# A fused scan and mixture-of-adapters kernel: the order of every engine written out instead of planned, and 17 instead of 21 gate products on GpSimd

## The chip, the cores and the metric

The kernel runs on one core of one Trainium2 chip. The metric is the device time of one execution in microseconds; lower is better. Five engines work side by side from their own instruction lists: TensorE (PE: matrix products and transposes), VectorE (DVE), ScalarE (ACT), GpSimd (POOL) and SyncE (SP, which here only starts transfers). They meet only at semaphores.

## What is computed

A recurrence over each of 8 sequences of 6400 steps, 128 channels wide, and then a small mixture of experts on its result; two of eight experts are taken for each of the 51,200 rows.

```python
h = a[:, t] * h + b[:, t]; out[:, t] = h          # the scan; x = out, as (51200, 128)
logits = x @ w_gate                               # (51200, 8)
topk = np.argpartition(-logits, 2, axis=1)[:, :2]
w = softmax of the two chosen logits
delta[rows with e chosen] += w * ((x @ A[e]) @ B[e])   # A: 128x16, B: 16x128 for each e
return x + delta
```

## The kernel before

The 51,200 rows are 100 units of 512 rows. Each unit goes through the same steps, which the code names by a letter and the number of the unit; in the profile they are found by line and tile:

- **AB** (TensorE, L86, pA and pB): 8 pairs of float32 transposes bring a unit of `a` and of `b` into PSUM with the channels on the partitions. At the edges a unit has a step A of its own for `a`.
- **aev** (ScalarE, L491): pA is copied to a_st. **scan** (VectorE, L510): one hardware scan over 512 columns, from a_st and pB into the ring xT (16 units). Units in which a new sequence starts are scanned in two pieces.
- **L** (TensorE, L82, into pTL): the logits, 4 matmuls with 8 columns. **Z** (L82, pZ): x times all 8 A side by side, 4 matmuls with 128 columns.
- The gating steps, for a group of units at once (mostly 4, fewer at both ends): **lev** (ScalarE, L583) copies the logits out, **mx** (L589) or **m1** and **m2** (L618, L646) on VectorE find the two largest, **p1** to **p7** (mostly GpSimd, L599 to L674) build the mask and the difference, **sig** (ScalarE, L684) is the sigmoid that gives the weights g.
- **mul** (L729): Z times the gate, into zw. On VectorE straight from PSUM; for some units on GpSimd, which then reads a copy **zev** (ScalarE, L715) of pZ in SBUF.
- **T** (TensorE, L86, pTL): 4 transposes of zw; **tev** (ScalarE, L786) copies them out. **R** (L82, pO from xT and ident_h): x itself is brought back to rows, 4 matmuls; **D** (L82, pO from zwT): plus zw times B.
- **oev** (L821): pO is copied to outt, on ScalarE, for some of the last 10 units on VectorE. **st** (SP): a store of 512 KB for two units, 256 KB for one.
- Loads **lda**, **ldb** (SP, L311), 512 KB for two units, go through rings of 8 slots each; a load may start when the AB steps that read its slot are done.

pA has one PSUM bank, pB, pZ and pO two each, pTL one that L and T share in turns. So AB of unit w waits for aev of unit w-1 and the scan of unit w-2, T of v for tev of v-1, R of v for oev of v-2.

What sets the order: every step is added to `_Plan` with a cost and a key (its unit plus an offset `KEY` by kind, L13). `schedule` (L108) is a list scheduler: it keeps a clock for each engine and takes, within a `SLACK`, the step with the smallest key. Its result is a fixed instruction list for each engine with the waits that the data and the buffers ask for. In the middle of the kernel that list repeats one pattern on TensorE, for each unit w:

```
AB(w) T(w-12) L(w-2) D(w-14) Z(w-9) R(w-13) AB(w+1) ...
```

`HOLD = 22` with `FREE = 100` ties the store of units u, u+1 to the scan of unit u+22, for u+22 below FREE (L847 to L851). `POOL_MULS = (2, 10, 4, 2)` puts mul of units 6, 10, 14 to 86 on GpSimd, 21 of them. TensorE's program is cut into parts of 243 instructions, with a branch in between (`_Parts`).

Of the kernel before, what the change touches and what calls it, by code (L numbers as in the profile page):

```python
# [12 lines left out]
KEY = {  # L13
    "AB": -228.9, "aev": 79.1, "scan": 140.1, "L": -12.2, "lev": -63.6, "gate": 83.5, "sig": 69.7, "Z": 27.8,
    "mul": -75.3, "zev": 6.2, "T": -117.7, "tev": 38.1, "R": 189.8, "D": 29.2, "oev": 168.4,
}
SLACK = {"pe": 20.0, "dve": 20.0, "act": 0.0, "pool": 60.0, "sp": 120.0}
# [3 lines left out]
POOL_MULS = (2, 10, 4, 2)  # L21
HOLD = 22
FREE = 100
HEATS = 7
WIDE = 100
SOLO = (2, 4)
FUSE = (100, 100)
WIDE8 = 460.0
# [4 lines left out]
FILLS = 0  # L33


class _Op:


    def __init__(self, name, engs, kind, unit, cost, emit, deps, dma, bank, mode):
        self.name = name  # L40
        self.engs = engs
        self.eng = engs[0]
        self.kind = kind
        self.unit = unit
        self.cost = cost
        self.emit = emit
        self.deps = deps
        self.dma = dma
        self.bank = bank
        self.mode = mode  # L50
        self.signal = False
        self.done = None
# [7 lines left out]


# [30 lines left out]
class _Plan:  # L92


    def __init__(self, sems, offset, slack):
        self.sems = sems
        self.offset = offset
        self.slack = slack
        self.ops = {}
        self.order = {e: [] for e in sems}  # L100

    def add(self, name, eng, kind, unit, cost, emit, deps=(), dma=None, bank=None, mode=None):

        engs = (eng,) if isinstance(eng, str) else eng
        cost = cost if isinstance(cost, dict) else {e: cost for e in engs}
        self.ops[name] = _Op(name, engs, kind, unit, cost, emit, list(deps), dma, bank, mode)

    def schedule(self, first, link, landing, switch):  # L108
        ops = self.ops
        users = {n: [] for n in ops}  # L110
        left = {}
        for op in ops.values():
            op.deps = [ops[d] for d in dict.fromkeys(op.deps) if d in ops]
            left[op.name] = len(op.deps)
            op.key = op.unit + self.offset.get(op.kind, 0.0)
            op.quick = min(c[0] for c in op.cost.values())
        for op in ops.values():
            for d in op.deps:
                users[d.name].append(op)
        begin, end = {}, {}  # L120
        cand = {e: [] for e in self.sems}
        free = {e: first for e in self.sems}
        bank = {}
        mode = None
        for op in ops.values():
            if not left[op.name]:
                for e in op.engs:
                    cand[e].append((0.0, op))
        todo = len(ops)
        while todo:  # L130
            found, soonest = [], {}
            for e, c in cand.items():
                for x in c:
                    op = x[1]
                    t = max(free[e], x[0])
                    if op.bank:
                        for o in bank.get(op.bank, {}).values():
                            if o.eng != e:
                                t = max(t, end[o.name])
                    if op.mode and mode and op.mode != mode:  # L140
                        t = max(t, free[e] + switch)
                    t += op.cost[e][0] - op.quick
                    found.append((t, op, e, x))
                    if t < soonest.get(e, 1e18):
                        soonest[e] = t
            e0 = min(soonest, key=soonest.get)
            limit = soonest[e0] + self.slack.get(e0, 0.0)
            t, op, e, pick = min((f for f in found if f[2] == e0 and f[0] <= limit), key=lambda f: (f[1].key, f[0]))
            t -= op.cost[e][0] - op.quick
            for x in op.engs:  # L150
                cand[x].remove(pick)
            op.eng = e
            mode = op.mode or mode
            if op.bank:
                held = bank.setdefault(op.bank, {})
                op.deps += [o for o in held.values() if o.eng != e]
                held[e] = op
            self.order[e].append(op)
            begin[op.name] = t
            free[e] = t + op.cost[e][0]  # L160
            if op.dma:
                ready = free[e] + 1000.0
                wait = max(0.0, link - ready)
                link = max(link, ready) + op.dma[2]
                end[op.name] = link + 300.0 + min(wait, landing(link))
            else:
                end[op.name] = t + op.cost[e][1]
            todo -= 1
            for u in users[op.name]:
                left[u.name] -= 1  # L170
                if not left[u.name]:
                    for x in u.engs:
                        cand[x].append((max(end[d.name] for d in u.deps), u))
        self.begin, self.end = begin, end
        self.span = max(end.values())
        for op in ops.values():
            for d in op.deps:
                d.signal = True
        for e, seq in self.order.items():
            n = 0  # L180
            for op in seq:
                if op.dma:
                    op.done = op.dma[:2]
                else:
                    n += op.signal
                    op.done = (self.sems[e], n)
# [18 lines left out]
def bass_associative_scan_2x2__then__mixture_of_adapters_kernel(  # L205
# [20 lines left out]
    lo, hi, every, at = POOL_MULS  # L226
    ON_POOL = lambda v: lo < v < NU - hi and v % every == at
# [22 lines left out]
    with ExitStack() as stack:  # L250
# [45 lines left out]
        s_cst = sb(nc.semaphore("s_cst"))  # L296
        dma_sem = {}

        plan = _Plan(sems, KEY, SLACK)
        add = plan.add  # L300

        def add_dma(name, eng, unit, starts, slot, time, deps=()):
# [11 lines left out]
            add(name, eng, "dma", unit, (450.0 * len(starts), 0.0), emit, deps, (sem, value, time))  # L314


        add("id0", "pool", "fix", -109, (200.0, 450.0), lambda h: h.memset(ident_f[:, :], 0.0))
# [3 lines left out]
            "fix",  # L321
            -109,
            (300.0, 400.0),
# [9 lines left out]
            ["id0"],  # L333
        )

        def cst_load(name, dst, src, after):

            sem = sb(nc.semaphore(f"s_{name}"))
            add(
                name,  # L340
                "act",
                "fix",
                -109,
                (450.0, 0.0),
                lambda h: h.dma_start(dst, src).then_inc(sem, 16),
                after,
                (sem, 16, 100.0),
            )
# [9 lines left out]
        add("w0", "dve", "fix", -109, (60.0, 200.0), lambda h: h.memset(warm[:, :], 0.0))  # L358
        add("table", "act", "fix", -108, (1500.0, 1600.0), lambda h: h.activation(warm[:, :], warm[:, :], ACTF.Sigmoid), ["w0"])
        add("wt", "dve", "fix", -109, (270.0, 400.0), lambda h: h.memset(warm_t[:, :], 0.0))  # L360
# [6 lines left out]
        add("heat", "pe", "fix", -109, (372.0 * HEATS, 372.0 * HEATS), heat, ["wt"], mode="half")  # L367

        def fill(w):


            def emit(h):
                for _ in range(2):
                    last = h.matmul(pO[1][:, :], warm_t[:, 0:128], warm_t[:, :])
                return last

            add(f"fill{w}", "pe", "fix", 1000.0, (440.0, 640.0), emit, [f"AB{w}"], mode="full")

        for w in range(FILLS):
            fill(w)  # L380
        add("idh", "dve", "fix", -108, (150.0, 330.0), lambda h: h.tensor_copy(ident_h[:, :], ident_f[:, :]), ["id"])
        add("cstg", "pool", "fix", -108, (190.0, 290.0), lambda h: h.tensor_copy(wg_h, cst_f[:, 0:E]), ["ld_g"])
        add(
            "cstA",
            "pool",
            "fix",
            -107,
            (290.0, 390.0),
            lambda h: h.tensor_copy(Acat_h, cst_f[:, E : E + 128]),
            ["ld_A"],  # L390
        )
        add(
            "cstB",
            "pool",
            "fix",
            -106,
            (290.0, 390.0),
            lambda h: h.tensor_copy(Bcat_h, cst_f[:, E + 128 : E + 256]),
            ["ld_B"],
        )  # L400
# [26 lines left out]
        def load(t, w):  # L427
# [3 lines left out]
            if many == 2 and n >= WIDE and n % 2 == 0 and w + 4 <= NU:  # L431
                many = 4
# [358 lines left out]
        def delta(v):  # L791
# [17 lines left out]
            if v == 1:  # L809
                deps += [f"fill{w}" for w in range(5)]  # L810
# [116 lines left out]
```

## Time and profile before

| | |
|---|---|
| median of 3 runs | 204.37 us (204.28 to 204.4) |
| the profiled execution, its own time | 204.88 us |
| its span, first to last instruction | 203.1 us |
| granted TensorE clock, mean | 0.989 |
| PE busy | 191.2 us, 3591 matmuls |
| DVE busy | 184.8 us, 268 instructions |
| ACT busy | 173.7 us |
| POOL busy | 115.7 us |
| moved by DMA | 79.35 MB, mean 391 GB/s |
| chain that ended last | PE 81%, DVE 6%, ACT 6%, DMA 2% |

"Span" leaves out 1.78 us of the execution that lie around the instructions. Matmuls overlap in the pipeline, so PE can be shown busy at every moment and still differ in how many it finishes; the count in a window, or the distance from start to start, tells more than its busy share. VectorE's and ScalarE's instructions overlap a little too (the next one starts while the last one ends), so what one costs in a full row is the distance from its start to the next start.

### The profile page before, as it was taken

To read this page: it belongs to the slowest core of one execution; us is meant where nothing else is said; L and a number is where in the kernel's file an instruction comes from. 1 tells how busy PE (TensorE), PEld (TensorE's weight loads), DVE (VectorE), ACT (ScalarE), POOL (GpSimd) and SP (SyncE) were. 2 spreads that over 40 slices of the span, in tenths; PEclk is the share of its full clock that TensorE was granted. 3 is DMA by queue.
4 is the path that set the end of the run, shared out by engine and by line. 5 is a ranking of instruction groups with operands and counts; after the bars stand their busy time and mean duration, and the time that the engine had idled before them with its cause. 6 is when DMAs were issued, how large, how long until landed. Compare 5 with 4: busy or idle time off the path is not lost.

```text
span 203.1 us, 8757 instructions
## 1 busy us (share of the span) xinstructions
PE 191.2 (94%) x3591; PEld 172.3 (85%) x3591; DVE 184.8 (91%) x268; ACT 173.7 (86%) x383; POOL 115.7 (57%) x244
## 2 busy tenths in 40 slices
PE   7788888999999999999999999999999999999992
PEld 3666777879899999999999999999999999999981
DVE  1579989999999999999999999999999999989970
ACT  3157686869899999989999999999999999999883
POOL 1324427568567466565656746656565687875520
PEclk9799999999999999999999999999999999999999
DMA  7999999999999999999999999999999999988867
GB/s 182 402 410 408 403 409 405 404 412 404 404 414 412 416 412 410 413 408 416 414 408 416 410 412 416 410 414 414 409 411 414 414 416 409 372 330 345 324 250 279
DMA packets 23688, 79.35 MB, mean 391 GB/s; under 512 B 3681, under 2 KB 3809, under 8 KB 23649
## 3 DMA queue, kind: packets, MB, share of 16 engines
q1 hardware_dynamic: 22320, 78.65, 97.0%
q8 instruction: 29, 0.48, 0.9%
q10 hardware_dynamic: 1328, 0.14, 0.5%
q14 instruction: 11, 0.08, 0.1%
HBM read 52.56 MB, written 26.21 MB: 388 GB/s over the span
## 4 chain that ended last, share of the span: by engine, by line
PE 81%; DVE 6%; ACT 6%; DMA 2%; issue 2%; POOL 1%; SPq 0%; DVEq 0%
PE pA L86 26%; PE pO L82 23%; PE pTL L86 14%; PE pZ L82 10%; PE pTL L82 5%; DVE xT L510 4%; PE pB L86 4%; DMA a_in<-in_a_dram 2%; ACT a_st L491 2%; ACT outt L821 2%; ACT zwT L786 1%; DVE mx L589 0%; SPq L311 0%; DVE zw L729 0%; ACT z_sb L715 0%
## 5 line engine op out<-in xcount | busy, mean ns | idle before, releaser
L510 DVE TENSOR_TENSOR_SCAN xT<-a_st,xT,pB 128x512 f16<-128x512 f32 x96 | 120.2, 1252 | 4.4 <-PE pZ L82 1.1
L491 ACT COPY a_st<-pA 128x512 f32<-128x512 f32 x100 | 60.6, 606 | 20.4 <-PE pB L86 15.7
L86 PE MATMUL pA<-ident_f,a_in 64*128 64x64 f32 (+1 forms) x792 | 71.8, 230 | 3.3 <-DMA a_in<-in_a_dram 1.1
L86 PE MATMUL pB<-ident_f,b_in 64*128 64x64 f32 (+1 forms) x792 | 72.5, 232 | 0.2
L86 PEld LDWEIGHTS pA<-ident_f,a_in 64*128 64x128 f32 (+1 forms) x792 | 58.0, 139 | 11.6 <-issue 2.4
L821 ACT COPY outt<-pO 128x512 f32<-128x512 f32 x96 | 59.5, 626 | 1.9 <-PE pO L82 1.7
L786 ACT COPY zwT<-pTL 128x512 f16<-128x512 f16 x95 | 58.4, 615 | 1.0 <-PE pTL L86 1.0
L86 PEld LDWEIGHTS pB<-ident_f,b_in 64*128 64x128 f32 (+1 forms) x792 | 58.0, 140 | 0.7 <-DMA b_in<-in_b_dram 0.4
L729 DVE TENSOR_TENSOR zw<-pZ,g 128x512 f16<-128x512 f32 x79 | 53.2, 679 | 2.1 <-PE pTL L86 1.2
L82 PE MATMUL pO<-ident_h,xT 128*128 128x128 f16 x400 | 41.2, 229 | 0.9 <-ACT outt L821 0.9
L82 PE MATMUL pZ<-cst_h,xT 128*128 128x128 f16 x400 | 38.6, 221 | 0.0
L86 PE MATMUL pTL<-ident_h,zw 128*128 128x128 f16 x380 | 37.7, 222 | 0.4 <-ACT zwT L786 0.4
L82 PE MATMUL pO<-cst_h,zwT 128*128 128x128 f16 x400 | 36.9, 218 | 0.6 <-ACT zwT L786 0.4
L82 PEld LDWEIGHTS pO<-ident_h,xT 128*128 128x128 f16 x400 | 32.8, 148 | 1.6 <-ACT outt L821 1.2
L729 POOL TENSOR_TENSOR zw<-z_sb,g 128x512 f16<-128x512 f32 x21 | 22.3, 1060 | 17.6 <-PE pTL L82 17.2
L82 PE MATMUL pTL<-cst_h,xT 128*128 128x8 f16 x400 | 27.9, 175 | 1.6 <-DVE xT L510 1.3
L82 PEld LDWEIGHTS pZ<-cst_h,xT 128*128 128x128 f16 x400 | 28.1, 115 | 0.2
L86 PEld LDWEIGHTS pTL<-ident_h,zw 128*128 128x128 f16 x380 | 21.8, 98 | 6.4 <-ACT zwT L786 0.5
L82 PEld LDWEIGHTS pTL<-cst_h,xT 128*128 128x128 f16 x400 | 23.6, 117 | 2.9 <-DVE xT L510 1.8
L625 POOL TENSOR_TENSOR d<-Lg,m 128x128 f32<-128x128 f32 (+3 forms) x29 | 10.7, 368 | 26.6 <-DVE m L618 26.5
L82 PEld LDWEIGHTS pO<-cst_h,zwT 128*128 128x128 f16 x400 | 23.9, 98 | 1.0 <-PE pO L82 0.9
L660 POOL TENSOR_SCALAR pn<-d 128x128 f32<-128x128 f32 (+3 forms) x31 | 17.3, 557 | 2.7
(36 smaller groups left out, 137.2 us busy)
## 6 DMA issues: line engine op xcount, KB each, us to landing
a_in<-in_a_dram SPq DMA_DIRECT2D x49, 512.0 KB, 13.7
b_in<-in_b_dram SPq DMA_DIRECT2D x49, 512.0 KB, 13.5
out_dram<-outt SPq DMA_DIRECT2D x47, 512.0 KB, 13.1
out_dram<-outt SPq DMA_DIRECT2D x6, 256.0 KB, 2.7
a_in<-in_a_dram SPq DMA_DIRECT2D x2, 256.0 KB, 9.2
b_in<-in_b_dram SPq DMA_DIRECT2D x2, 256.0 KB, 4.3
cst_f<-in_moe_A_dram ACTq DMA_DIRECT2D x1, 64.0 KB, 4.0
cst_f<-in_moe_B_dram ACTq DMA_DIRECT2D x1, 64.0 KB, 5.0
```

What stands on the lines that cost most here:

```text
L82: return self.h.matmul(*args, **kw)
L86: return self.h.transpose(*args)
L491: lambda h: h.copy(a_st[w % 2][:, :], pA[0][:, :]),
L510: last = h.tensor_tensor_scan(out=x_at(lo, hi), data0=a_st[w % 2][:, lo:hi], data1=pB[w % 2][:, lo:hi], initial=init, op0=ALU.mult, op1=AL ...
L625: lambda h: h.tensor_tensor(out=v(d1[s]), in0=v(Lg[s]), in1=bc(m1[s]), op=ALU.subtract),
L660: lambda h: h.tensor_scalar(v(pn[s]), v(d2[s]), 0.0, -1.0e30, ALU.is_lt, ALU.mult),
L729: lambda h: h.tensor_tensor(out=oview, in0=zview, in1=gview, op=ALU.mult),
L786: lambda h: h.copy(*evacuated(v)),
L821: return copy(outt[:, v % NOUT, :], pO[v % NO][:, :])
```

## The change

The planner goes. Each engine's order is written out as a string, one letter for a step (`CODES`); steps of one kind are taken by rising unit. The order in which T/tev and L/lev share the bank pTL is written as well (`BANKS`), and so is which steps go to VectorE where there is a choice (`ELSE`). What is computed, the tiles and their sizes stay. Cut to its core:

```diff
-KEY = {"AB": -228.9, "aev": 79.1, "scan": 140.1, ...}
-SLACK = {"pe": 20.0, "dve": 20.0, "act": 0.0, "pool": 60.0, "sp": 120.0}
-POOL_MULS = (2, 10, 4, 2)
-FREE = 100
-SOLO = (2, 4)
+CODES = dict(zip("bdfkpqrvhyBCEijAacsLZuTtRDozlx41567gm23nwe",
+    "idz id ld_g ld_A ld_B w table wt heat idh cstg cstA cstB lda ldb A AB aev scan L Z mul T tev R D oev zev lev mx p4 p1 p5 p6 p7 sig m1 p2 p3 m2 st end".split()))
+ORDERS = {
+    "pe": """
+        hAaAaLaLRaZaLLTaZZLaLRaDTaZaLLDTLaZTZaRRDaTDRaLLLRLaZTZaDDLaRTZaLRLTLaZZDDTLaZRTaZDLTRaLDZTRaLTZRaTL
...
+    "dve": """
+        qvyssxsx157susxsmususmnsusnmsusnsusmsusnsusmusunsussumususnsusmsusnsusumsusnsusumsususnsusmususnussm
...
+    "act": """
+        fpkccrlclcgcglcltcglctcocltcgotcoctgoclcgtzcooctcltgcotcotcztocotgcltctooctocztlcogoctctoctocltgoczt
...
+    "sp": """
+        ijijjijijiiijjjjjiiiiijjjiijiiijjjjiijwijjiwijwijwjwjwwjjjiiiiwjiijwiiwiwwwwwjjjjwjiwwjiwiijijwwwiij
+        ijijijjjjjiiwwjwiwjwiiwwijjiwwwijiwwwwwwwwwwwwwwwwwwwe
...
+ELSE = "oev90 oev93 oev95 oev97 oev98 p5_0 p7_0 p1_1".split()
+POOL_MULS = (7, 12, 17, 22, 27, 32, 37, 42, 47, 52, 57, 62, 67, 72, 77, 82, 87)
+FREE = 90
+PAIRS = (2, 98)
+SINGLE = 2
...
-    def schedule(self, first, link, landing, switch):
...
+    def arrange(self):
+        ops = list(self.ops.values())
+        for op in ops:
+            op.deps = [self.ops[d] for d in dict.fromkeys(op.deps) if d in self.ops]
+        self.order = {e: self.pick(ORDERS[e], [op for op in ops if op.eng == e]) for e in self.sems}
+        for name, codes in BANKS.items():
+            held = {}
+            for op in self.pick(codes, [op for op in ops if op.bank == name]):
+                op.deps += [o for e, o in held.items() if e != op.eng]
+                held[op.eng] = op
...
-    ON_POOL = lambda v: lo < v < NU - hi and v % every == at
+    ON_POOL = lambda v: v in POOL_MULS
...
-            deps = [f"aev{w - 1}", f"scan{w - 2}", "id"]
+            deps = [f"aev{w - 1}", f"scan{w - 2}", "id", "heat"]
...
-            stores.append((u, len(mates(u))))
-            u += stores[-1][1]
+            n = 2 if u < NU - SINGLE else 1
+            stores.append((u, n))
+            u += n
```

In the built programs both have 3591 matmuls. VectorE gets four products more (83 instead of 79) and five of the last output copies instead of four; ScalarE loses four copies of pZ and one output copy. ScalarE's list has one table load more: before, the load for the sigmoid and a one-column sigmoid stand ahead of all copies; after, a table load stands ahead of aev0 and the one for the sigmoid, with that one-column sigmoid, stands between aev1 and lev0. Units 96 and 97 become a pair, and stores 0 to 50 replace 0 to 52.

In the middle of the kernel TensorE's list no longer repeats one pattern: between two AB steps there are three to seven others, in changing order (`AB34 Z25 R21 T23 D20 AB35 D21 Z26 T24 R22 AB36 D22 Z27 L33 T25 L34 R23 AB37`).

More of the change, by code (lines that the diff above doesn't have):

```diff
@@ L108, in schedule @@
-    def schedule(self, first, link, landing, switch):
[L109 to L176, printed above, removed]
```

282 lines of the change are left out of this document (100 added, 182 removed).

## The prediction

> **What bounds the kernel now.** I read the table of stretches first, then the order of starts on TensorE and VectorE in the middle, then both ends. The stretches are from and to, length, then PE, PEld, DVE, ACT, POOL busy us with counts, granted clock, DMA share, GB/s:
>
> ```profile
> 0.00:20.00 20.00, 15.78 (x201) 11.81 (x203) 12.40 (x35) 9.13 (x22) 5.33 (x24) 0.91 0.95 349
> 20.00:40.00 20.00, 17.48 (x338) 15.03 (x335) 19.06 (x26) 14.62 (x33) 10.34 (x26) 1.00 1.02 405
> 40.00:60.00 20.00, 19.42 (x377) 17.46 (x378) 19.60 (x27) 17.21 (x39) 13.45 (x24) 1.00 1.03 408
> 60.00:160.00 100.00, 99.96 (x1989) 92.35 (x1986) 97.90 (x128) 95.64 (x209) 62.24 (x111) 1.00 1.03 412
> 160.00:180.00 20.00, 20.00 (x398) 18.50 (x398) 19.57 (x31) 19.33 (x48) 15.37 (x39) 1.00 0.99 396
> 180.00:204.00 24.00, 18.56 (x304) 17.15 (x304) 16.27 (x26) 17.79 (x39) 8.94 (x23) 0.96 0.74 289
> ```
>
> From 60 to 180 TensorE is never idle and finishes 2387 matmuls in 120 us, 19.9 per us; a unit has 36, so a unit takes 1.81 us. In the first 60 us it finishes 916, which at that rate are 46 us of work: 14 us are missing, the start before the first data among them. From 180 on, 304 matmuls are 15.3 us of work. So TensorE sets the pace of the middle, and what an order can win lies in the first 60 us and in the last 20. VectorE is busy 95 to 98% from 20 us on, so in the first part it is VectorE that TensorE waits for.
>
> Start by start, one unit on TensorE (AB, T, L, D, Z, R, next AB):
>
> ```profile
> 80.16 0.27 PE L86 MATMUL pA<-ident_f,a_in 64*128 64x64 f32 x1
> ...
> 80.81 0.40 PE L86 MATMUL pTL<-ident_h,zw 128*128 128x128 f16 x4
> 81.04 0.28 PE L82 MATMUL pTL<-cst_h,xT 128*128 128x8 f16 x4
> 81.17 0.38 PE L82 MATMUL pO<-cst_h,zwT 128*128 128x128 f16 x4
> 81.39 0.39 PE L82 MATMUL pZ<-cst_h,xT 128*128 128x128 f16 x4
> 81.62 0.41 PE L82 MATMUL pO<-ident_h,xT 128*128 128x128 f16 x4
> 81.96 0.27 PE L86 MATMUL pA<-ident_f,a_in 64*128 64x64 f32 x1
> ```
>
> AB 0.65, T 0.23, L 0.13, D 0.22, Z 0.23, R 0.34: 1.80 us, with no idle time in a row. Another order of the same steps has the same sum: one AB per unit means one change from float32 to float16 and one back.
>
> VectorE in the middle:
>
> ```profile
> 87.53 1.27 DVE L510 TENSOR_TENSOR_SCAN xT<-a_st,xT,pB 128x512 f16<-128x512 f32 x1
> 88.73 0.69 DVE L729 TENSOR_TENSOR zw<-pZ,g 128x512 f16<-128x512 f32 x1
> 89.34 0.28 DVE L618 TENSOR_REDUCE m<-Lg 128x16 f32<-128x128 f32 x1
> 89.54 1.27 DVE L510 TENSOR_TENSOR_SCAN xT<-a_st,xT,pB 128x512 f16<-128x512 f32 x1
> ```
>
> In a full row a scan takes 1.20, a product 0.61, a maximum 0.20 us. Per unit: 1.20 + 0.75 x 0.61 + 2 x 0.20 / 4 = 1.76 us before. After, 4 of 5 products are on VectorE: 1.20 + 0.80 x 0.61 + 0.10 = 1.79 us. Both are just below TensorE's 1.80.
>
> **The change, part by part.** The steps are the same; I go through the time in three stretches and sum what each loses or wins. The rows of the first stretch (VectorE's mx_0, which stands between scans 0 and 1, then scans 2, 7, 15 and 29; ScalarE's table load and aev2; TensorE's R0 and the start of AB2):
>
> ```profile
> 8.07 0.37 DVE L589 MAX8 mx<-Lg 128x8 f32<-128x8 f32 x4 [1.25 <-ACT Lg L583]
> ...
> 11.08 1.28 DVE L510 TENSOR_TENSOR_SCAN xT<-a_st,xT,pB 128x512 f16<-128x512 f32 x1 [1.13 <-PE pZ L82]
> ...
> 19.81 1.28 DVE L510 TENSOR_TENSOR_SCAN xT<-a_st,xT,pB 128x512 f16<-128x512 f32 x1
> ...
> 34.14 1.27 DVE L510 TENSOR_TENSOR_SCAN xT<-a_st,xT,pB 128x512 f16<-128x512 f32 x1
> ...
> 58.40 1.27 DVE L510 TENSOR_TENSOR_SCAN xT<-a_st,xT,pB 128x512 f16<-128x512 f32 x1
> ```
>
> ```profile
> 2.29 1.28 ACT L359 ACT_TABLE_LOAD   x1 [2.29 <-issue]
> ...
> 10.41 0.58 ACT L491 COPY a_st<-pA 128x512 f32<-128x512 f32 x1 [2.36 <-PE pB L86]
> ```
>
> ```profile
> 8.68 0.64 PE L82 MATMUL pO<-ident_h,xT 128*128 128x128 f16 x4
> 9.25 0.37 PE L86 MATMUL pA<-ident_f,a_in 64*128 64x64 f32 x1
> ```
>
> *First stretch, to scan 29.* The new order puts B1 ahead of L0 and AB2 ahead of R0 and Z0 (in the old one both stand before AB2), and scan 1 ahead of mx_0. So scan 1 no longer waits behind mx_0 (0.37 us), and AB2 starts up to 0.8 us sooner (R0 from 8.68 to 9.25, and Z0 before it). Against that stands the table load between aev1 and lev0: ScalarE was idle there for 2.36 us ahead of aev2, and 1.28 fits in that, so most of it is covered; lev0 is some 1.5 us later, and mx_0 now has scan 1 ahead of it anyway. I get scan 2 at about 10.4 instead of 11.08. Three short gate steps (p1_1, p5_0, p7_0) then stand ahead of scan 3, and mul 2 ahead of scan 7, so by scan 7 little of that is left: 0.2 us, plus one product that is already done.
>
> From there VectorE is the bound, and I count its list in a full row. From scan 7 to scan 15 the old list took 14.3 us (19.81 to 34.14) with 5 products; the new one has 8 scans, 4 products and 7 short maxima: 9.6 + 2.4 + 0.9 = 12.9 us. From scan 15 to scan 29 the old took 24.3 us with 9 products; the new one has 14 scans, 10 products and 7 maxima: 16.8 + 6.1 + 1.4 = 24.3 us in a full row. Without any gap scan 29 starts at 58.4 - 0.2 - 1.4 = 56.8. Some gaps will stay; bounds 0 and -1.6, and I take **-1.3** us, near the full row, because TensorE, at 338 matmuls in 20 us against 398, has room there.
>
> *Second stretch, scan 29 to scan 99.*
>
> ```profile
> 58.40:188.00 129.60, 129.56 (x2553) 119.75 (x2552) 126.36 (x171) 124.06 (x275) 83.01 (x162) 1.00 1.01 405
> ```
>
> Before: 58.40 to 188.01, 129.6 us (the row is the table's for this stretch), 1.85 per unit, which is TensorE's 1.80 and the branches between its parts. VectorE's new list between these two scans is 70 scans, 58 products (55 before), 42 maxima: 84.0 + 35.4 + 8.2 = 127.6 us, so it still fits, with 2 us to spare instead of 4. TensorE has four steps fewer ahead of AB99 (48 instead of 44 behind it), -0.9 us. ScalarE loses three of the copies of pZ. On the other side, waits get tighter. Counted in the two lists in units of one AB to the next, R stands at least 1.03 units behind the copy that frees its bank before and 0.67 after, T 2.67 units behind its product before and 1.62 after, D 1.17 behind its tev before and 0.68 after. Between 30 and 180 us TensorE waits on such a copy twice, 0.3 us each:
>
> ```profile
> PE pA L86 <- ACT zwT L786: 0.6, 2, 0.4
> ```
>
> Three such waits cost the 0.9 that is won. I take **0** for this stretch; the ends are -0.9, and +3.6 if a dozen places pay 0.3.
>
> The four products that leave GpSimd cost VectorE 4 x 0.61 = 2.4 us and the fifth output copy 0.6; they are in these counts. What GpSimd gains nobody waits for: it is busy 62 of the 100 us from 60 to 160.
>
> *Third stretch, from scan 99.* Scan 99 and product 98 on VectorE:
>
> ```profile
> 188.01 1.28 DVE L510 TENSOR_TENSOR_SCAN xT<-a_st,xT,pB 128x512 f16<-128x512 f32 x1
> ...
> 196.05 1.29 DVE L729 TENSOR_TENSOR zw<-pZ,g 128x512 f16<-128x512 f32 x2 [0.74 <-ACT g L684]
> ```
>
> Product 98 starts 8.0 us after scan 99, having waited 0.74 for the sigmoid, which stood behind two tev in ScalarE's list. In the new list it stands behind one less, and VectorE has scan, 6 products, 3 output copies and 2 maxima between: 1.2 + 3.7 + 1.8 + 0.3 = 7.0 us. The copy of unit 98 goes to VectorE, off ScalarE's chain. TensorE's 48 steps at 0.225 need 10.8 us of the 15 that are there. I take **-1.0**; bounds -1.5 and +0.5, since 0.9 us of TensorE's work has moved behind AB99. The last store is 256 KB in both.
>
> *Transfers.* Moved bytes are equal. Loads are written in bursts now: some stand in SP's list behind one that waits for a much later AB. Before, each load is issued 15 units (27 us) ahead of its AB; after, some only 8 (lda45 behind ldb52, ldb58 behind st14), which is 14.4 us.
>
> ```profile
> DMA to landing us min/median/max: 3.0/13.7/17.7
> ```
>
> The median would just do; and while SP holds back, the queue runs down, so a burst lands sooner than the median. A transfer of 512 KB at 412 GB/s takes 1.27 us: AB37 comes near 70 us (scan 29 at 57 and 1.85 per unit); by then SP's list has issued about 55 transfers of that size, and (70 - 2) / 1.27 = 53 are served, so lda45 has three or four ahead of it. I cost this at 0. Freed stores (`FREE`) come when the share of DMA is already falling to 0.74, and nobody waits for them.
>
> *Sum:* -1.3 + 0 - 1.0 = -2.3 us. The profiled execution, 204.88 (203.1 and 1.78 around it), would be 202.6; it stands 0.5 above the median, so 204.37 - 2.3 = **202.1 us**.
>
> The Trainium skill, page "ScalarE: Activation LUTs", section "What ACT_TABLE_LOAD costs", speaks against one part: a switch to another table set costs about 2.66 us, 1.283 for the load and about 1.38 for a drain. The row above agrees with the first figure (1.28); a load between two copies no run here shows. By the page, as an estimate, lev0 and aev2 would start near 10.9, scan 2 near 11.5, and the sum would be about -1.3.
>
> **Rivals.**
> - *The middle pays for its tight waits* (slower). TensorE's irregular order has less room behind each copy and product; wherever one is late, TensorE stands still, and in the middle nothing gives that back. At 0.3 us each it takes 8 such waits among 70 units to eat 2.3 us; at 20, one in 3 or 4 units, the time is 202.1 + 6 = 208, at 12 it is 205.7. For it: the counted distances. Against it: a distance of 0.67 units is 1.2 us, and a copy takes 0.6.
> - *The second table load holds ScalarE longer.* If a pause as long as the load (1.28) follows it, aev2 starts near 11.0 and scan 2 near 11.6 instead of 10.4; what VectorE loses there nothing returns before scan 29: -2.3 + 1.2 = -1.1, 203.3. For it: ScalarE has to finish aev1 before the load and nothing else stands in the 2.36 us. Against it: the first load takes 1.28 in its row, and the copies that follow aev1 are short.
> - *VectorE becomes the bound.* Its 127.6 us plus the 3.2 us by which it was not busy in the second stretch (129.6 - 126.4) make 130.8, +1.2: 203.3. If the first stretch also wins nothing, 204.4, no change. For it: 98% busy. Against it: its idle time there came from TensorE.
> - *Late loads* (slower). If the bursts land like the latest ones, 17.7 - 14.4 = 3.3 us at each of the two places: 208.7. Decides if the queue is as full at AB37 as in the middle of before.
> - *Both ends do better and the middle wins its four steps:* -1.6 - 0.9 - 1.3 = -3.8, 200.6.
>
> **How the numbers follow.** Forecast 0.41 (201.2 to 203.0). Both ends and the middle better 0.14. Table load 0.08. VectorE as the bound 0.12, of which 0.07 end within 0.4 us of before. Tight waits 0.19, late loads 0.06. Two runs of this kernel can tell apart about 0.2%, 0.4 us. Faster 0.41 + 0.14 + 0.08 + 0.05 = 0.68; the same 0.07; slower 0.19 + 0.06 = 0.25. The range reaches from 200.0, just past the better case, to 205.8, the dozen waits.
>
> **What would show it.** Right: scan 29 starts near 57 and scan 99 near 186.7, with 398 matmuls per 20 us between; product 98 about 7 us after scan 99. Wrong: fewer than 395 matmuls per 20 us in the middle with rows of waits of TensorE on ScalarE or VectorE; AB steps that wait for a_in or b_in; a gap on ScalarE behind the second table load beyond 1.28; scan 29 no sooner than 58.

## The result: slower, and the profile after

The changed kernel takes 206.58 us (median of 20 runs, 204.95 to 207.96) against 204.38 us for the kernel before (20 runs, 204.21 to 206.72): ratio 1.0091, 95% interval [1.0061, 1.012]. The forecast was 202.1. All ratios and intervals here are worked out from the runs within 1.5% of the fastest of their kernel, the medians from all runs, so a ratio is not the quotient of the two medians beside it.

The profiled run of the changed kernel took 207.92 us, span 206.1, mean granted clock 0.971; it lies 1.3 us above its median, so its losses are a little too large. Its line numbers are others: L114 and L118 are before's L82 and L86, L431 is L510. Its table of stretches, columns as in the prediction:

```profile
0.00:20.00 20.00, 15.84 (x154) 11.29 (x155) 10.77 (x31) 7.98 (x17) 4.79 (x22) 0.74 0.93 342
20.00:40.00 20.00, 18.41 (x351) 15.89 (x349) 19.42 (x29) 15.29 (x36) 11.06 (x29) 1.00 1.03 407
40.00:60.00 20.00, 19.68 (x385) 17.77 (x382) 19.43 (x26) 18.29 (x39) 11.82 (x22) 1.00 0.99 361
60.00:160.00 100.00, 99.11 (x1956) 90.49 (x1956) 97.22 (x128) 93.82 (x200) 57.55 (x105) 1.00 1.03 408
160.00:180.00 20.00, 20.00 (x397) 18.47 (x393) 19.70 (x31) 19.47 (x46) 14.23 (x34) 1.00 1.03 412
180.00:207.00 27.00, 21.84 (x370) 20.21 (x367) 19.81 (x33) 20.72 (x47) 12.70 (x33) 0.95 0.76 302
```

TensorE finishes 154 matmuls in the first 20 us where before finished 201: at 19.9 per us that is 2.4 us of work. The next two rows give back 21 of these 47, the long row from 60 to 160 us loses 33 again. The clock is 0.74 there, 0.91 before.

The scans 2, 7, 15 and 29 on VectorE, which the prediction used as marks:

```profile
11.57 1.28 DVE L431 TENSOR_TENSOR_SCAN xT<-a_st,xT,pB 128x512 f16<-128x512 f32 x1 [0.85 <-PE pO L114]
...
22.18 1.27 DVE L431 TENSOR_TENSOR_SCAN xT<-a_st,xT,pB 128x512 f16<-128x512 f32 x1
...
35.44 1.27 DVE L431 TENSOR_TENSOR_SCAN xT<-a_st,xT,pB 128x512 f16<-128x512 f32 x1
...
60.21 1.27 DVE L431 TENSOR_TENSOR_SCAN xT<-a_st,xT,pB 128x512 f16<-128x512 f32 x1
```

Scan 7 comes 2.4 us later than before (19.81). From 7 to 15 the new list needs 13.3 us against 14.3 (12.9 were counted); from 15 to 29 24.8 against 24.3. So the loss is made ahead of scan 7.

One reason: the written order of ScalarE starts the loads g, B, A; before it was g, A, B. The transfers of the constants, with KB and us to landing, first in before, then after:

```profile
cst_f<-in_moe_A_dram ACTq DMA_DIRECT2D x1, 64.0 KB, 4.0
cst_f<-in_moe_B_dram ACTq DMA_DIRECT2D x1, 64.0 KB, 5.0
```

```profile
cst_f<-in_moe_B_dram ACTq DMA_DIRECT2D x1, 64.0 KB, 3.6
cst_f<-in_moe_A_dram ACTq DMA_DIRECT2D x1, 64.0 KB, 11.2
```

A lands at about 13 us instead of 5. On GpSimd (the cast of A, and the gate step behind it) and on TensorE (Z0) after:

```profile
12.94 0.29 POOL L334 CAST cst_h<-cst_f 128x128 f16<-128x128 f32 x1 [1.89 <-DMA cst_f<-in_moe_A_dram]
13.19 0.25 POOL L502 TENSOR_TENSOR d<-Lg,mx 128x32 f32<-128x32 f32 x1
```

```profile
13.29 0.61 PE L114 MATMUL pZ<-cst_h,xT 128*128 128x128 f16 x4 [0.64 <-POOL cst_h L334]
```

Z0 started at 8.26 before. The gating steps of GpSimd queue behind the cast as well. With A loaded first (e1 below) the cast still starts 5 us later than the 5.2 of before, since GpSimd's written list has a gate step ahead of it; Z0, at 11.63, did not wait for it there:

```profile
10.46 0.29 POOL L334 CAST cst_h<-cst_f 128x128 f16<-128x128 f32 x1
```

Scan 2 is 0.5 us later than before, and ahead of it AB2 waited for a load of `b`:

```profile
9.74 0.34 PE L118 MATMUL pA<-ident_f,a_in 64*128 64x64 f32 x1 [0.72 <-DMA b_in<-in_b_dram]
```

In the three traces in which A landed 10.1 us after its issue or later (after, e10, e15) scan 2 started at 11.57 to 12.01, in the eleven others of the written order at 10.13 to 11.00. Which of the two late transfers holds back the other no run shows.

The chain that ended last, after, shows that transfer, and TensorE with 88% instead of 81%:

```profile
PE 88%; DMA 5%; ACT 3%; issue 2%; ACTq 0%; DVE 0%; POOL 0%
PE pA L118 28%; PE pO L114 26%; PE pZ L114 13%; PE pTL L118 11%; PE pTL L114 6%; DMA cst_f<-in_moe_A_dram 5%; PE pB L118 4%; ACT a_st L412 1%; ACT outt L685 1%; ACTq L311 0%; DVE zw L608 0%; ACT zwT L656 0%; ACT z_sb L602 0%; POOL cst_h L334 0%; ACT g L574 0%
```

The other end. The start of the last AB and of the last four matmuls on TensorE, before and then after:

```profile
187.26 0.71 PE L86 MATMUL pB<-ident_f,b_in 64*128 64x64 f32 x8
...
198.92 0.40 PE L82 MATMUL pO<-cst_h,zwT 128*128 128x128 f16 x4
```

```profile
189.20 0.71 PE L118 MATMUL pB<-ident_f,b_in 64*128 64x64 f32 x8
...
202.20 0.38 PE L114 MATMUL pO<-cst_h,zwT 128*128 128x128 f16 x4 [0.22 <-ACT zwT L656]
```

From the last AB TensorE needs 11.66 us before and 13.00 after: 1.34 more. The lists have 42 and 48 steps there, and six steps of 0.225 are 1.35. The span ends 4.2 and 3.9 us behind the start of TensorE's last step.

So I cut the spans at scan 29 and at the last AB. This is the table to which the experiments are held (us, from the profiled runs):

| | to scan 29 | to the last AB | to the end | span |
|---|---|---|---|---|
| before | 58.40 | 128.86 | 15.84 | 203.1 |
| after | 60.21 | 128.99 | 16.90 | 206.1 |
| forecast of the difference | -1.3 | 0 | -1.0 | -2.3 |
| difference | +1.8 | +0.1 | +1.1 | +3.0 |

The forecast had cut at scan 99, not at the last AB. Scan 99 after:

```profile
191.59 1.27 DVE L431 TENSOR_TENSOR_SCAN xT<-a_st,xT,pB 128x512 f16<-128x512 f32 x1
```

At that mark the three differences are +1.8, +1.8 and -0.6 us. In the written order scan 99 starts 2.4 us behind the start of the last AB, before 0.75, so the mark itself moves 1.6 us from the third stretch into the second. Since the chain that ended last runs over TensorE, the table cuts at TensorE's last AB.

Single profiles differ at the start by about as much as is sought: in e7 and e18, whose orders differ from before's at most in the two constants, scan 29 started at 57.51 and 57.65, where the profile of before has 58.40.

### The profile page after: what moved, and what is told of

Read it like the earlier page. It is cut to its first block, busy times and chain, and to the rows that moved or that the text cites. A ratio compares the mean times of both kernels' runs of the same rounds, so it can differ in the third digit from the quotient of the medians.

```text
span 206.1 us, 8810 instructions
## 1 busy us (share of the span) xinstructions
PE 194.9 (95%) x3591; PEld 174.1 (84%) x3591; DVE 186.4 (90%) x272; ACT 175.6 (85%) x379; POOL 112.2 (54%) x241
## 4 chain that ended last, share of the span: by engine, by line
PE 88%; DMA 5%; ACT 3%; issue 2%; ACTq 0%; DVE 0%; POOL 0%
PE pA L118 28%; PE pO L114 26%; PE pZ L114 13%; PE pTL L118 11%; PE pTL L114 6%; DMA cst_f<-in_moe_A_dram 5%; PE pB L118 4%; ACT a_st L412 1%; ACT outt L685 1%; ACTq L311 0%; DVE zw L608 0%; ACT zwT L656 0%; ACT z_sb L602 0%; POOL cst_h L334 0%; ACT g L574 0%
## 5 line engine op out<-in xcount | busy, mean ns | idle before, releaser
L431 DVE TENSOR_TENSOR_SCAN xT<-a_st,xT,pB 128x512 f16<-128x512 f32 x96 | 120.2, 1252 | 5.9 <-PE pO L114 1.3
L118 PE MATMUL pA<-ident_f,a_in 64*128 64x64 f32 (+1 forms) x792 | 74.1, 235 | 3.1 <-ACT a_st L412 0.9
L118 PE MATMUL pB<-ident_f,b_in 64*128 64x64 f32 (+1 forms) x792 | 74.2, 235 | 1.2 <-issue 0.8
L118 PEld LDWEIGHTS pA<-ident_f,a_in 64*128 64x128 f32 (+1 forms) x792 | 59.5, 143 | 12.4 <-issue 2.4
L118 PEld LDWEIGHTS pB<-ident_f,b_in 64*128 64x128 f32 (+1 forms) x792 | 59.4, 143 | 2.3 <-issue 1.3
L685 ACT COPY outt<-pO 128x512 f32<-128x512 f32 x95 | 56.8, 603 | 2.0 <-PE pO L114 1.6
L608 DVE TENSOR_TENSOR zw<-pZ,g 128x512 f16<-128x512 f32 x83 | 55.5, 674 | 2.0 <-PE pZ L114 1.9
L114 PE MATMUL pO<-ident_h,xT 128*128 128x128 f16 x400 | 42.0, 231 | 0.2 <-ACT outt L685 0.2
L114 PE MATMUL pZ<-cst_h,xT 128*128 128x128 f16 x400 | 39.1, 224 | 0.6 <-POOL cst_h L334 0.6
L118 PE MATMUL pTL<-ident_h,zw 128*128 128x128 f16 x380 | 37.6, 220 | 0.5 <-DVE zw L608 0.3
L114 PE MATMUL pO<-cst_h,zwT 128*128 128x128 f16 x400 | 37.1, 219 | 0.3 <-ACT zwT L656 0.2
L114 PEld LDWEIGHTS pO<-ident_h,xT 128*128 128x128 f16 x400 | 32.6, 149 | 1.9 <-ACT outt L685 0.4
L114 PEld LDWEIGHTS pZ<-cst_h,xT 128*128 128x128 f16 x400 | 27.3, 116 | 3.0 <-POOL cst_h L334 0.8
L114 PEld LDWEIGHTS pO<-cst_h,zwT 128*128 128x128 f16 x400 | 24.5, 98 | 2.2 <-PE pO L114 0.3
L118 PEld LDWEIGHTS pTL<-ident_h,zw 128*128 128x128 f16 x380 | 24.4, 98 | 1.9 <-issue 0.8
L525 POOL TENSOR_TENSOR d<-Lg,m 128x128 f32<-128x128 f32 (+3 forms) x29 | 10.7, 371 | 27.7 <-DVE m L519 26.6
L114 PE MATMUL pTL<-cst_h,xT 128*128 128x8 f16 x400 | 25.1, 174 | 0.5 <-issue 0.2
L608 POOL TENSOR_TENSOR zw<-z_sb,g 128x512 f16<-128x512 f32 x17 | 18.1, 1063 | 13.0 <-ACT z_sb L602 7.7
L114 PEld LDWEIGHTS pTL<-cst_h,xT 128*128 128x128 f16 x400 | 21.6, 117 | 2.0 <-issue 0.5
L549 POOL TENSOR_TENSOR d<-Lg,m 128x128 f32<-128x128 f32 (+3 forms) x29 | 10.8, 371 | 19.3 <-DVE m L543 19.1
## 6 DMA issues: line engine op xcount, KB each, us to landing
cst_f<-in_moe_A_dram ACTq DMA_DIRECT2D x1, 64.0 KB, 11.2
```

The lines of the kernel that those rows point to most:

```text
L114: return self.h.matmul(*args, **kw)
L118: return self.h.transpose(*args)
L431: last = h.tensor_tensor_scan(out=x_at(lo, hi), data0=a_st[w % 2][:, lo:hi], data1=pB[w % 2][:, lo:hi], initial=init, op0=ALU.mult, op1=AL ...
L525: lambda h: h.tensor_tensor(out=v(d1[s]), in0=v(Lg[s]), in1=bc(m1[s]), op=ALU.subtract),
L549: lambda h: h.tensor_tensor(out=v(d2[s]), in0=v(Lg[s]), in1=bc(m2[s]), op=ALU.subtract),
L608: add(f"mul{v}", eng, lambda h: h.tensor_tensor(out=oview, in0=zview, in1=gview, op=ALU.mult), deps)
```

## The experiments

All times are medians; each ratio is to the kernel before on the same chip (its median was 204.3 to 204.4 each time).

### The start: order of the constants, and the table load

e1, A ahead of B (the letters `k` and `p` in ScalarE's string: ld_A and ld_B):

```diff
-fpkccrlclcgcg...
+fkpccrlclcgcg...
```

> The changed kernel with the load of A issued ahead of that of B, as before the change (two letters of ScalarE's list). Theory of the start: in the changed kernel A lands 11.2 us after its issue instead of 4.0, GpSimd's cast of A and with it Z0 wait until 12.9, and TensorE idles and runs at half its clock from 10 to 20 us. With A first, A lands about 4 us after issue, scan 7 starts near 20.5 instead of 22.2, and the time falls by 1 to 2 us, to about 205. Rival (only the middle matters): the start's delay is absorbed later, the time stays within 0.5 us of 206.6.

205.93 us, ratio 1.0082 [1.0052, 1.0112]. A lands 4.2 us after its issue, scan 2 starts at 10.55 instead of 11.57, and scan 29 at 58.82 instead of 60.21. By the medians it is 0.65 us, less than expected, and the two intervals overlap nearly whole: alone, this edit's gain is not shown.

e8, besides A first, the table load ahead of aev0:

```diff
-fpkccrlclcgcg...
+fkprcclclcgcg...
```

> The changed kernel with A ahead of B, as e1, and the second table load ahead of aev0 instead of between aev1 and lev0. Theory 'the table load stands in the path': ScalarE waits for the first data there anyway, so lev0 and the first gates come 1 us sooner than in e1, and the time is 205.0 to 205.5. Rival 'the 2.36 us of idle time covers it': 205.9 as e1.

205.78, 1.0071 [1.0036, 1.0106]. 0.15 under e1, within both spreads: the load between aev1 and lev0 was nearly covered, as forecast. ScalarE's rows in the changed kernel show that nothing follows the load but its own 1.28 us:

```profile
8.13 0.59 ACT L412 COPY a_st<-pA 128x512 f32<-128x512 f32 x1 [1.93 <-PE pA L118]
8.74 1.28 ACT L322 ACT_TABLE_LOAD   x1
10.03 0.20 ACT L322 ACTIVATE warm<-warm 128x1 f32<-128x1 f32 x1
```

The Trainium skill, page "ScalarE: Activation LUTs", section "What ACT_TABLE_LOAD costs", gives 1.38 us more for a drain; this row does not show it: 8.74 + 1.28 = 10.02, and the next instruction starts at 10.03.

e7, the reverse test: before with B loaded ahead of A (the two calls of cst_load exchanged, and GpSimd's casts with them).

> The kernel before with the load of B issued ahead of that of A on ScalarE's queue, and GpSimd's two casts in that order; nothing else moved. Theory 'late A': A lands several us later than the 4.0 us of before, Z0 and so the product 0 and what hangs on it come later, and the time goes up by 0.5 to 1.5 us (204.9 to 205.9). Rival: the planned order has L, R and further AB to do meanwhile; no change (204.0 to 204.8).

208.66, 1.0155 [1.0087, 1.0223], but the six runs are 204.65, 206.65, 207.75, 209.56, 209.76 and 214.28. The median is above what the theory asked for; with this spread the test does not settle it. Its profile is of the run of 204.65, in which A landed after 5.8 us, in time for Z0 at 8.20. Whether A was later in the longer runs no profile shows.

### Bursts of loads

e5: e1 with an even list on SyncE (an lda and an ldb in turn, later a store after each pair). e10: the same list in the changed kernel, with A behind B. e11: even list, A first and table load early, the three together.

```diff
-ijijjjijijiiijjjjjiiiiijjjiijiiijjjjiijwijjiwijwijwjwjwwjjj...
+ijijjjijijijijijijijijijijijijijijijijijijwijwijwijwijwijwijw...
```

> The changed kernel with A loaded ahead of B (as in e1, 205.93) and with SyncE's list made even: one lda, one ldb in turn, then a store after each pair, about as in before, instead of bursts. Theory 'bursts': what is still lost between 60 and 120 us (20 to 30 matmuls against before) comes from transfers that run in bursts, so the loss goes: about 205.0, with 395 or more matmuls in every 20 us from 60 on. Rival 'the order of the compute engines': SyncE's list has nothing to do with it, 205.9 as e1, and the stall of 0.8 us near 62 us may stay or move.

> The changed kernel with SyncE's list made even, as in e5, and A left behind B. Theory 'bursts': 0.6 us less, as from e1 to e5, about 206.0, and a narrower spread of the runs. Rival 'the late A hides it': what is waited for at the start is A and the clock, so 206.5 as the changed kernel.

> A ahead of B, the table load ahead of aev0, and SyncE's list even. If the three are separate causes, their single effects add: 206.58 - 0.65 (A) - 0.15 (table) - 0.57 (loads) = 205.2. Rival 'one cause in three shapes' (whatever lets TensorE stand still at the start lowers its clock): no better than e5, 205.4.

e5: 205.36, 1.0027 [0.9996, 1.0059]; e10: 206.63, 1.0094 [1.0061, 1.0128]; e11: 205.11, 1.001 [0.9984, 1.0036]. With A first the even list wins 0.6 to 0.7 us in the medians twice (e1 to e5, e8 to e11), though the intervals of each pair overlap or touch; with A late it wins nothing. The clear step is e10 to e11, 1.5 us with intervals apart: with even loads, A first and the early table load together are worth that. No AB waited for a load in the middle of the changed kernel; what stands out there is one row, 0.8 us inside an AB at a border between two parts of TensorE's program:

```profile
63.24 0.27 PE L118 MATMUL pB<-ident_f,b_in 64*128 64x64 f32 x1 [0.82 <-issue]
```

It is not there in e5, e10 and e11, whose middle stretch is 127.9 us in all three, 1.1 less. But e15 below keeps the bursts, and its middle stretch is 127.8: that bursts of loads delay the fetching of the program is not shown. The intervals of e5 and e11 take in 1, so neither can be told from before, though e11's median is still 0.7 us over it: of the 2.2 us that were lost, 1.5 hang on the three repairs. What is left in its profile:

| | to scan 29 | to the last AB | to the end | span |
|---|---|---|---|---|
| e11 less before | +0.9 | -1.0 | +1.05 | +1.0 |
| e13 less before (below) | +0.2 | -0.9 | +1.1 | +0.4 |

TensorE's 13.0 in the end is the same in every kernel with the written order (12.9 to 13.1), and the end as a whole is 16.87 to 16.98 us wherever the last stores land 2.0 us after their issue. In e9, e12, e14 and e15 below they take 3.3 to 3.8, and the end is 18.15 to 18.85; e12 and then e13:

```profile
out_dram<-outt SPq DMA_DIRECT2D x2, 256.0 KB, 3.8
```

```profile
out_dram<-outt SPq DMA_DIRECT2D x2, 256.0 KB, 2.0
```

What the middle wins in e11 and e13, the end pays back.

### The place of R

In the changed order R stands directly ahead of an AB 28 times; before, in most units. e2 moves R to the end of its gap between two ABs; e3 is e2 with A first and the table load early; e4 makes the converse in before (R ahead of Z):

```diff
+ORDERS["pe"] = _r_last(ORDERS["pe"])
```

```diff
+        pe = self.order["pe"]
+        for i in range(len(pe) - 2):
+            if [o.kind for o in pe[i : i + 3]] == ["Z", "R", "AB"]:
+                pe[i], pe[i + 1] = pe[i + 1], pe[i]
```

> The changed kernel with R moved to the end of its gap between two AB steps wherever its own D is not in that gap: 62 instead of 28 R then stand right ahead of an AB. Theory of R's place: from the starts in both traces, R costs 0.30 us ahead of a float16 step and the step ahead of AB then pays 0.10 for the change of type, while R itself ahead of AB costs 0.35 in all; so 0.05 us for each of 34, -1.7 us, about 204.9. Rival (tight waits): R was placed where its bank is free, later or earlier makes no difference to TensorE's sum; the time stays within 0.5 us or grows, since D and the copies behind R come later.

> The changed kernel with R last as in the run before, the load of A ahead of B, and the table load for the sigmoid moved from behind aev1 to ahead of aev0. If the place of R and the start are both causes, the gains add: 206.6 - 1.7 - 1.5 - 0.3 = about 203.1, below the kernel before (204.4). If only one of them is a cause, 205; if neither, 206.6.

> The kernel before, where TensorE's list has Z, R, AB now R, Z, AB: 72 times R no longer stands right ahead of AB, nothing else changes. Theory of R's place: 72 x 0.05 = 3.6 us slower, about 208, with R to Z at 0.30 and Z to AB at 0.32 instead of 0.22 and 0.35. Rival, and what the prediction assumed (the sum of TensorE's steps does not depend on their order): within 0.4 us of 204.4.

e2: 209.19, 1.0213 [1.0195, 1.0232]; e3: 207.59, 1.0142 [1.0125, 1.0159]; e4: 205.05, 1.004 [1.0017, 1.0062]. The theory fell. R in another place costs TensorE next to nothing by itself: in e4 R to Z and Z to AB take 0.25 + 0.32 (medians), in before Z to R and R to AB 0.22 + 0.35. The rival's 0.4 us was missed as well: e4 is 0.65 us slower, under 0.01 for each of the 72 places. Moving R in the written order lost 2.6 us (e2) and 1.8 (e3 against e8). Between 30 and 186 us e2's view of waits has 1.2 us on steps of VectorE, ScalarE and GpSimd that the changed kernel does not have; the rest of the loss is not attributed.

### The 17 products

```diff
-POOL_MULS = (2, 10, 4, 2)
+POOL_MULS = (2, 10, 5, 2)
```

> The kernel before, its planner unchanged, with the 17 gate products of the changed kernel on GpSimd (units 7, 12, ... 87) instead of 21. Theory 'VectorE has no room': 4 more products on VectorE, 2.4 us, show as a loss of 1 to 2.4 us (205.4 to 206.8), since VectorE is about 97% busy in the middle. Rival 'TensorE sets the pace': within 0.4 us of before (204.0 to 204.8), and the written order, not the count of products, is the cause of the slowdown.

215.5 (213.56 to 217.6), 1.0506 [1.0451, 1.0561]: beyond both. The planner turned its regular pattern into an irregular one (two Z or two R of different units side by side), so this does not price the products. VectorE is busy 87% of that run. The count of products under an unchanged order wasn't tried.

### The clock at the start

In the changed kernel the clock is at half from 9.7 to 20 us. Before had it too, from 7.6 to 11.0 (columns as in the table of stretches):

```profile
8.00:10.00 2.00, 2.00 (x25) 1.74 (x25) 1.82 (x6) 0.04 (x1) 1.03 (x4) 0.50 1.02 410
```

The window from 10 to 20 us, after, e11 and e13:

```profile
10.00:20.00 10.00, 8.94 (x123) 7.44 (x121) 7.94 (x27) 4.26 (x14) 3.89 (x15) 0.50 1.03 408
```

```profile
10.00:20.00 10.00, 9.31 (x128) 7.59 (x125) 8.63 (x28) 4.55 (x13) 4.66 (x17) 0.51 1.02 407
```

```profile
10.00:20.00 10.00, 8.45 (x148) 6.11 (x145) 9.45 (x29) 5.29 (x15) 4.67 (x17) 1.00 1.03 409
```

e9, e12, e13 and e15 put 8 matmuls that nobody reads into TensorE's gaps (F):

```diff
-hAaAaLaLRaZaLLTaZZ...
+hAaFAaLFaLRaZFaLFLFTaZZ...
+        for i, n in enumerate((1, 2, 1, 3, 1)):
+            add(f"F{i}", "pe", fill(n), ["wt"])
```

> The changed kernel with 8 more matmuls on TensorE that nobody reads (warm_t into the bank pZ1, ahead of Z1), put where TensorE stands idle in the first 14 us: 1, 2, 1, 3 and 1 of them, each about 0.2 us. Theory 'clock': the idle time at the start makes TensorE's clock fall to half for some 10 us, and the runs' times rise with what is missing of the granted clock (0.26 us per 0.01 in the changed kernel); with the gaps filled the clock stays at 0.99 or more, and the time is 205.8 to 206.1. Rival 'VectorE paces the start': the clock may rise, but the time stays at 206.4 to 206.8, or rises by up to 1.6 us, the time of the fillers.

> As e11, with the fillers of e9. Theory 'clock': granted clock 0.99 or more and 204.4 to 204.7, the lowest times of e5 (204.60 at 0.991). If the written order holds a gain of its own behind the losses at the start, as forecast for the first and the third stretch, below 204.2; rival 'no gain in the order': 204.4 or more, whatever the start does.

e9: 209.1, 1.019 [1.0132, 1.0247]; e12: 207.29, 1.0123 [1.0079, 1.0167]. The clock did come back (0.997, 0.996), and in e12 scan 29 started at 57.16, where the prediction had put it; but neither kept it. e12 was still 0.6 us ahead of before at the last AB (186.65 against 187.26), e9 0.4 behind (187.67); behind it each lost 3.0 us, in part by the late stores shown above. The fillers had also moved every border between the parts of TensorE's program (243 instructions each) by 16 instructions. e13 (on e12) and e15 (on e9) make the first part 16 longer, so that the borders stand between the same steps as in the changed kernel:

```diff
-PART0 = 172
+PART0 = 188
```

> As e12 (three repairs and fillers), and the first part of TensorE's program 16 instructions longer (PART0 188), so that all later borders between parts stand between the same steps as in e11 and the changed kernel. e12 was 2.1 us ahead of before at 60 us and lost it again up to 180, while its borders had moved by the 8 fillers. Theory 'borders': a border costs more inside an AB than between float16 steps, and the written order was made with its borders in place; with them back, what is won at the start stays: 203.0 to 204.2. Rival 'fed too early': the lead of the start has nowhere to go, TensorE's full row in the middle is the bound either way, and it ends as e12, 207.3. Rival 'the middle's own loss': as e11, 204.4 to 205.1.

> The changed kernel with the fillers of e9 and its borders kept in place (PART0 188). Theory 'borders': e9 without its loss after 60 us, and with the clock at 0.99: 205.7 to 206.2, under the 206.58 of the changed kernel, which prices the clock at 0.4 to 0.9. Rival: the fillers cost what the clock wins, 206.4 to 207, or as e9, 209.1.

e13: 204.97, 1.0024 [0.9998, 1.005]; e15: 207.52, 1.0118 [1.0087, 1.0148]. From scan 2 to scan 7 the traces with before's order take 8.73 us (before, e7, e16, e18). The written order takes 9.37 where the clock is full there (e3, e9, e12, e13, e15), 10.24 to 10.26 at half clock with A in time (e1, e5, e8, e11, e17), and 10.61 and 10.88 at half clock with A late (after, e10). So 0.6 is the order's own (it has one product more there, 0.61), half clock costs 0.9, and the late A 0.4 to 0.6. With the 0.5 of scan 2 that makes the 2.4 us lost ahead of scan 7.

In the times of the runs the clock is less plain. Within e13 the six runs with a mean clock of 0.998 or more took 204.29 to 204.65, the six below 205.29 to 206.74. But three of the 20 runs of the changed kernel had a clock of 1.0 and took 206.51, 206.80 and 206.85, about its median. And fillers are no sure gain: e13 is 0.14 under e11, and e15, with A late, 0.9 over the changed kernel. What the clock is worth in the medians stays open.

The Trainium skill, page "TensorE: Matmul & The Clock Gate", Part 1, says that the clock falls to half after one idle window of about 3.4 us. The half clock agrees (0.50), and so does the length: summed from the granted clock, the stretches of half clock last 3.4 us in before, 6.8 in e8, 10.2 in after, e1 and e11, and 13.7 in e5. The cause agrees only loosely, since TensorE never stood idle for more than about 1 us between 6 and 10 us of the changed kernel, and was busy 1.19 and 1.09 of 2 us there.

### The borders of TensorE's program

e14 is e11, e16 is before, both with PART0 156; e17 is e11, e18 is before, both with 188.

> As e11 (three repairs, 205.11), with nothing but the borders moved: the first part 16 instructions shorter (PART0 156), so that every border stands as in e12. Theory 'borders': the loss of e12 between 60 and 180 us, 1.5 to 2.2 us, comes without any filler: 206.6 to 207.3. Rival: the fillers did it, 205.1 as e11.

> The kernel before, with nothing but the borders moved by 16 instructions (PART0 156). Theory 'borders': before's place of them is one of several, and the time is off by up to 2 us, 205 to 206.5. Rival 'only the tight written order feels them': its pattern repeats, so the borders walk through it anyway, 204.2 to 204.8.

> As e11 (three repairs, no filler, 205.11), with the first part of TensorE's program 16 instructions longer (PART0 188): every border stands 8 matmuls later in the written order, and at the same addresses as in e13 (204.97). Theory 'the place among the steps counts' (from e12, 207.29, against e13): the borders stand at other steps than the order was made with, 205.8 to 207.3. Rival 'the place in memory counts' (from e14, where the parts moved the other way and the time rose by 91 us): the parts lie as in e13, so 204.8 to 205.3 as e11 and e13, and e12's loss stays open.

> The kernel before with the first part 16 instructions longer (PART0 188). In e16, 16 shorter, TensorE stood still for 4 to 5 us at many borders, 284 us. Theory 'a part must be fetched as a whole': longer is as harmless as in e13, 204.2 to 204.8. Rival 'any move of the parts hurts': over 210.

e14: 296.03, 1.4343 [1.427, 1.4416]; e16: 283.98, 1.3861 [1.3805, 1.3918]; e17: 205.23, 1.0029 [1.0005, 1.0053]; e18: 204.8, 1.0012 [0.9987, 1.0037]. No theory had foreseen what 16 instructions less do. TensorE's longest waits in e16 (us in total, times, longest):

```profile
PE pB L86 <- issue: 12.2, 5, 4.4
PE pZ L82 <- issue: 12.2, 3, 5.2
PE pO L82 <- issue: 8.9, 3, 5.0
PE pA L86 <- issue: 5.7, 6, 1.8
PE pTL L82 <- issue: 5.3, 1, 5.3
PE pTL L86 <- issue: 4.1, 1, 4.1
```

"issue" is a wait for nothing that the profile shows, up to 5 us each. The Trainium skill, page "Runtime: NRT & Kernel Launch", section "Instruction fetch mechanics", says that a taken branch whose target is not in the fetched pages has to wait for a transfer of that page; the rows fit that. Why 156 meets it and 172 and 188 do not isn't shown. e17 speaks against the theory that borders inside the steps cost much: other steps, 205.23. So e12's loss against e13, 2.3 us by PART0 alone, stays open: the place among the steps, the place in memory, or the two together. Where it lies can be said: of the 2.0 us between the two spans, -1.4 lie ahead of scan 29, +1.5 between it and the last AB, and +1.9 behind it, where TensorE's part is 13.1 and 13.0 and the last stores land later. For e9 against e15, the pair with A third, the middle has +1.9 and the end +0.7.

No version beats the kernel before. The intervals of e5, e11, e13 and e18 take in 1; their medians are 0.5 to 1.0 us above it.

## Why the prediction was wrong, step by step

- *What bounds the kernel.* Right, but not thought through. "Another order of the same steps has the same sum" held: from 80 to 180 us a unit takes TensorE 1.82 us in both orders. What is late at scan 29 stays late: in e5, e10, e11, e13 and e17 the middle takes 127.9 to 128.0 us, whether scan 29 starts at 58.6 or at 61.2. And TensorE bounds the end as well, which the prediction left out.
- *First stretch, -1.3.* **This step failed**: +1.8. It failed ahead of scan 7, where the prediction said "0.2 us": it got -2.4. Against the 19.6 of the forecast scan 7 is 2.6 us late: scan 2, at 11.57 instead of 10.4, makes 1.2 of it, the half clock 0.9 and the late A 0.4. The load of A behind B the prediction didn't look at, because it counted SyncE's transfers only; the clock it took as full. VectorE's list from scan 7 on was counted to 0.9 us (13.3 us against 12.9, with six maxima where the prediction counts seven, and 24.8 against 24.3): it won 0.6 of the 1.4. With A first, even loads and a full clock (e12) scans 2, 7 and 29 came at 10.24, 19.61 and 57.16, near the forecast 10.4, 19.6 and 57. So the count fits a start that this kernel doesn't have; and measured against e18's 57.65 it would be a gain of 0.5, not of 1.3.
- *The table load.* Right: covered (e8, 0.15 and within the spread). Scan 2 did come at 11.57, near the 11.5 and 11.6 of the prediction's estimate by the Trainium skill and of the rival, but that is luck: aev2, the next copy, waited for AB2, which had waited for its data.
- *Second stretch, 0.* To the last AB right by its size (+0.1), in its parts not; to scan 99, the prediction's own mark, +1.8. With even loads the way to the last AB wins 0.9 to 1.0, from nine steps fewer between AB29 and AB99 (434 and 425; six stand behind AB99, three ahead of AB29), less than the 2.0 that nine steps are worth. The 0.8 at 63 us ate most of it.
- *Third stretch, -1.0.* **Failed** behind the last AB: +1.1. From scan 99, its own mark, it is -0.6, with product 98 7.7 us behind scan 99 (199.29) against 8.0 before and 7.0 forecast; but scan 99 itself is later by more than that wins. The prediction counted 44 and 48 steps behind the last AB; they are 42 and 48. And it had them covered ("10.8 us of the 15 that are there"), although TensorE is what ends the kernel: its 48 steps took 13.0.
- *Tight waits.* Between 30 and 180 us the view of waits of the changed kernel lists for TensorE three of "issue", 1.2 us together, and none on a copy, a scan or a product. The rival was wrong, though the times that it gives (205.7 to 208) take in the 206.58: that is luck too.
- *Late loads.* In the middle no AB waited for SyncE's transfers. The late loads are at the start: a constant of 64 KB on ScalarE's queue, and `b` for AB2 (0.72 us).
- *VectorE as the bound.* Not shown; e6 could not settle it.

The sign came from the two ends, cut at scan 29 and the last AB: forecast -2.3 together, measured +2.9 in the profiled run. About 1.5 of the 2.2 us of the medians are mended by e11's three edits; the rest, +1.0 in e11's profile, is the sum of the start (+0.9), the middle (-1.0) and the end (+1.05). No run mended the end, so its part rests on the count of steps alone.

## What to carry to other kernels

Where one engine is in a full row until the end, moving its steps from ahead of the last input to behind it wins nothing: count them on both sides and check that the engine has idle time there. When an order is written out, look at every queue of it in the first microseconds, the small constants too: one load of 64 KB exchanged with its neighbour landed 7 us later here, and putting it back, together with an early table load and with even loads, won 1.5 us (e10 to e11). And any edit that adds instructions to a program cut into parts must be measured with the cuts in mind.

## What the runs showed of the hardware that was not expected

- A load of 64 KB (A, 128x8x16) landed 3.9 to 5.1 us after its issue as the second of three on its queue. As the third, when the large loads were under way, it took 5.8, 6.9, 7.2, 10.1, 11.2 and 11.6 in the six traces that have it (e7, e2, e9, e15, after, e10); B, as large but with longer rows, took 5.0 to 6.0 as the third.
- TensorE's clock can fall to 0.50 for 10 us without an idle time over about 1 us, and its stretches at half clock lasted 3.4, 6.8, 10.2 or 13.7 us; the runs of e13 differ by about 1 us with the clock, three runs of the changed kernel at 1.0 do not differ from its median.
- A first program part of 156 instead of 172 instructions costs 80 to 91 us (e16, e14), in waits of up to 5.3 us at no event.
